# New quad orders in an attention block, and a scaled bias that stays in its tile until the MLP

## The chip, the core and the metric

The kernel runs on one core of one Trainium2 chip. The metric is the device time of one execution in microseconds; lower is better. Below, PE is TensorE's matmul stream, PEld its weight loads, DVE is VectorE, ACT is ScalarE, POOL is GpSimd and SP is SyncE, which issues nearly all DMAs.

## The reference

A transformer block over 2048 tokens of 576 channels: adaptive layer norm, attention with 32 query heads of 18 channels that share one key and one value head, then adaptive layer norm and an MLP of 4608 hidden channels with its own layer norm, all in float32.

```python
mod = (_silu(c) @ w_mod).reshape(c.shape[0], 6, 1, -1)
h = _layernorm(x) * (1 + ca) + sa
x = x + ga * attention(h)        # softmax(q k^T * 18**-0.5) v, then @ wo
h = _layernorm(x) * (1 + cb) + sb
x = x + gb * (gelu(_layernorm(h) @ w1 + b1) @ w2 + b2)
```

## The kernel before

Three stages follow each other: projections to q, k and v (until about 130 us), attention (until about 1372 us), and the MLP.

**Attention** works in 32 **quads**: quad n is four heads over one quarter of the queries (512 tokens). For each quad the kernel needs the scores (S), their row maxima, the exponential, the product with V and a normalisation. Each step that makes a bank of PSUM is one 64-row matmul of 512 columns, and there are two kinds:

- S tokens (`st_mm`, L941): a score matmul; ACT takes its exponential into P (L943).
- M, X and R tokens (`mx_mm`, L327 and L951): they find the row maxima of the quad that comes next. An M bank is reduced by DVE (L963); an X bank goes through a ReLU on ACT (L954) and is combined with an R bank on DVE (L961).

The matmuls are 64 rows high, so the array holds two of them; the digit of a token (0 or 1) is the half that it uses. Matmuls of different halves run side by side, those of one half one after the other. X and R always use half 1. A quad issues 64 S, 48 M, 8 X and 8 R.

Seven banks stand in a ring (`bank`, L80): a token takes the oldest bank, one with a plus sign the second oldest, one with two the third oldest. A matmul into a bank waits until ACT or DVE has read what was there.

V tokens (`pv_mm`, L921) are the products with V: a V token with the number g issues g parts, each of four 32-column matmuls of 128 columns, into the eighth bank, psC. They lag eight parts behind the scores; the last parts of a quad are therefore among the first of the next quad's order. When they are done, `post_quad` (L742) begins with a copy of psC to the tile O on ACT (L747). Its other steps are tokens of the next quad's order:

- T1: DVE transposes O to T (L750).
- RC: DVE takes the reciprocals (L753), POOL multiplies T by them (L754).
- T2: DVE transposes T back to O (L756).
- OS: ACT rounds O into the tile os (L766), POOL writes the remainder (L767), and SP sends both to the operand of the output projection.

O, T and os have one buffer each. The token F1 finishes the maxima of the next quad, F2 transposes them on PE (L365) and sends them to the queries of the next quad.

**The order is written by hand as a string of tokens**: QUAD for quads 0 to 8, QUADW for 9 to 30, LAST for 31. QUADW has one token more, WO: a piece of the output projection (14 matmuls on PE, L732, and an addition on DVE, L736). After every four parts of V the function `between` (L967) gives POOL steps of a preparation of the MLP's weights (L800 to L883) and, every second time, a step of a queue `fill`, which holds the second layer norm. Two steps of that norm are PE transposes (L163) and run only behind a WO, which happens in every second quad from 12 to 26. Three groups of four parts per quad, those ahead of F2 and RC, get no preparation steps.

The second bias, scaled (`load_b2` L634, `b2_scaled` L639), is made once in the attention, for the layer norm of the first two token blocks (L626), in a tile of the pool px. That pool is closed after the attention; the MLP opens a new one and makes the bias again for the other two blocks: a load ahead of its first step (L1112) and the two POOL operations of `b2_scaled` inside step v = 0 (L1421).

Of the kernel before, what the change touches and what calls it, by code (L numbers as in the profile page):

```python
# [8 lines left out]
F32 = mybir.dt.float32  # L9
# [5 lines left out]
S, D, H, DH, F = 2048, 576, 32, 18, 4608  # L15
# [17 lines left out]
def block_kernel(ctx: ExitStack, tc, x, wqkv, wo, w1, b1, w2, b2, c, wmod, ident_in, out):  # L33
# [3 lines left out]
    per = ctx.enter_context(tc.tile_pool(name="per", bufs=1))  # L37
# [27 lines left out]
    def big(): return per.tile([128, 10, 512], F32R, name="big", bufs=3)  # L65
# [387 lines left out]
    for tb in range(NB):  # L453
        nz = big() if tb + 1 < NB else None
        for i, m in enumerate((4, 0, 1, 2, 3)):
# [42 lines left out]
    px = pxp.__enter__()  # L498
# [4 lines left out]
    WO, YR, ATT, B2 = {}, {}, {}, {}  # L503
# [128 lines left out]
        yield  # L632

    def load_b2():  # L634
        b2g = px.tile([128, D], F32, name="b2g")
        sy.dma_start(b2g, b2.to_broadcast([128, D]))
        return b2g

    def b2_scaled(b2g):  # L639
        po.tensor_mul(b2g, b2g, BC[:, 2, :])  # L640
        po.tensor_scalar(b2g, b2g, 2.0, None, op0=ALU.mult)
        return b2g
# [99 lines left out]
    def post_quad(n, PV):  # L742

        tb, qd = divmod(n, NQ)
        e = po if n < NQT - 1 else ve
        O = px.tile([128, TB], F32, name="O")
        ac.activation(O, PV, AF.Copy)  # L747
        yield
        T = px.tile([128, 16, 32], F32, name="T")
        ve.transpose(T.rearrange("p a b -> p (a b)"), O)  # L750
        yield
        R = px.tile([128, 16], F32, name="R", bufs=2)
        ve.reciprocal(R, T[:, :, DH])  # L753
        e.tensor_tensor(T, T, R[:, :, None].to_broadcast([128, 16, 32]), op=ALU.mult)  # L754
        yield
        ve.transpose(O, T.rearrange("p a b -> p (a b)"))  # L756
        yield
        if tb not in ATT:
            assert tb
            ATT[tb] = big()  # L760
        A = ATT[tb].rearrange("p (s k) t -> p s k t", s=2)
        if n == NQT - 1:
            os = A[:, :, KD - 1, :]
        else:
            os = px.tile([128, 2, TB], F32R, name="os")
        ac.activation(os[:, 0], O, AF.Copy)  # L766
        e.tensor_tensor(os[:, 1], O, os[:, 0].bitcast(F32), op=ALU.subtract)  # L767
        if qd < NQ - 1:
            for j in range(4):
                k, r = divmod(4 * qd + j, HC)  # L770
                sy.dma_start(A[DH * r:DH * (r + 1), :, k, :].bitcast(F32), os[32 * j:32 * j + DH].bitcast(F32))
        elif n < NQT - 1:
            for j in range(4):
                sy.dma_start(A[DH * j:DH * (j + 1), :, KD - 1, :].bitcast(F32),
                             os[32 * j:32 * j + DH, :1].bitcast(F32).to_broadcast([DH, 2, TB]))
            for j in range(4):
                r = 4 + j % 3
                sy.dma_start(A[DH * r:DH * (r + 1), j // 3, KD - 1, :].bitcast(F32), os[32 * j:32 * j + DH, 1].bitcast(F32))
# [114 lines left out]
    QUAD = """S0+ M0 S1 S1+ M0 V3 S0 M1 S1+ M0 M1++ S0 V3 M0 S1+ M1 S0+ V2 M0 S1+ S1 M0+ X1 S0+ V4 T1 X1 M0 M1 M0
            S1 S0 V4 S1 RC M0+ S1 S0 M0+ S0+ M1 V3 S0 M1 R1 S1+ S0 M0+ X1 V3 M0 S1 S1+ R1 S0 M0 S1 V3 M0+ X1 M0
            S0 S1 S0 M1 V3 M0+ S1 S1+ M0 S0 R1+ S0 V3 R1+ S0 S1 M1 S0 M0 X1 V3 M0+ S1 M0 S1 S0 S0 R1 V3 M0+ X1
            S0+ M1 S0 M1+ V3 S1 M0+ M0 S1 T2 S0 S1 V4 M0 S1 S0 M1+ S0 M1 V3 S0 R1+ S1 M0 F1 S1 S0 V3 X1 M0 S1 M0
            R1 S0 F2 OS V4 M0+ M1 S0+ S1 M0+ X1 V4 S1 M0 S1+ S0 M1 M0+ S1 V2 R1 S0 M1 S0+ V2 S0 S1 M0 M1 V2 S1""".split()
# [443 lines left out]
    fill = deque([ln2_pair()])  # L1341
# [20 lines left out]
    for v in range(NV):  # L1362
# [6 lines left out]
        def more(half="", first="", room=False):  # L1369

            if v in (0, NG - 1, NG):
                form(first if v == 0 else half if v == NG - 1 else {"+T4": "-T4 +T1 -B22", "-T4": "-T1 -t1"}.get(first, ""))
            elif v > NG + 1 and fill:
                step(fill)
            elif 0 < v < NG and fill and (room or mark[0] != "T" or v == NG - 2):
                mark[0] = next(fill[0], "end")
                if mark[0] == "end":
                    fill.popleft()
            if v == 0 and rest:
                for _ in range(2):  # L1380
# [140 lines left out]
```

## Time and profile before

| | us |
|---|---|
| median of 3 runs | 2222.11 (2221.9 to 2223.86) |
| profiled execution, own time | 2223.82 |
| its span, first to last instruction | 2221.7 |
| PE busy | 2201.1 (99%) |
| DVE busy | 1927.8 (87%) |
| ACT busy | 1644.4 (74%) |
| POOL busy | 1525.1 (69%) |

The shares are averages over stages with different limits. PE's busy time counts matmuls in the pipeline, with modelled ends, so a busy PE is not PE at its peak. The granted clock of TensorE is 1.00 of its higher level, 2.4 GHz, in every quad shown below. Quads are found in the trace by ACT's copy of psC to O, which runs once in each; the time from one to the next is called the period.

### The profile page before, as it was taken

What the parts mean: (1) busy time and instruction counts of PE and PEld (TensorE: products, weight loads), DVE (VectorE), ACT (ScalarE), POOL (GpSimd) and SP (SyncE); (2) the same over time, 40 slices, a digit from 0 to 9 for tenths busy, and PEclk for the clock granted to TensorE, in tenths of its full rate; (3) what the DMA queues carried; (4) which work ended last, traced back from release to release, by engine and by line L of the source; (5) the groups of instructions that cost most, each with busy time, mean ns of one, the idle gap of its engine ahead of it and who ended that gap; (6) DMA issues with size and microseconds to landing.
All of it is one profiled execution on the core that took longest, in us unless ns stands there. A gap on an engine that the chain in (4) does not pass through costs nothing.

```text
span 2221.7 us, 46258 instructions
## 1 busy us (share of the span) xinstructions
PE 2201.1 (99%) x16814; PEld 1457.5 (66%) x16814; DVE 1927.8 (87%) x3417; ACT 1644.4 (74%) x3145; POOL 1525.1 (69%) x1761
## 2 busy tenths in 40 slices
PE   8999999999999999999999999999999999999999
PEld 6655555444544545445454456888888898989898
DVE  7589999999999999999999983888888878888887
ACT  5569999999999999999999998444445444343443
POOL 6654455766776786687686630988888867877776
PEclk9999999999999999999999999999999999999999
DMA  6232143433333333342333322666666646676664
GB/s 231 84 132 92 34 134 117 140 128 109 125 117 120 124 124 108 102 140 94 116 130 112 130 70 69 204 178 175 177 181 179 184 131 182 179 219 188 178 184 124
DMA packets 183880, 308.01 MB, mean 139 GB/s; under 512 B 18815, under 2 KB 74511, under 8 KB 183653
## 3 DMA queue, kind: packets, MB, share of 16 engines
q1 hardware_dynamic: 183509, 304.91, 44.1%
q8 instruction: 133, 2.18, 0.4%
q14 instruction: 94, 0.77, 0.1%
q10 hardware_dynamic: 144, 0.15, 0.0%
HBM read 200.97 MB, written 93.79 MB: 133 GB/s over the span
## 4 chain that ended last, share of the span: by engine, by line
PE 88%; POOL 2%; DVE 2%; ACT 1%; issue 1%; DMA 0%; POOLq 0%; ACTq 0%
PE psC L931 22%; PE psB L1159 18%; PE psA L1262 16%; PE bk L941 15%; PE bk L327 10%; PE bk L732 2%; PE bk L951 2%; PE psA L1296 1%; DVE mx L963 1%; ACT P L943 1%; PE psA L732 0%; POOL r L801 0%; PE psB L256 0%; POOL r L862 0%; DVE mx L352 0%
## 5 line engine op out<-in xcount | busy, mean ns | idle before, releaser
L943 ACT ACTIVATE P<-bk 128x512 f32<-128x512 f32 x2048 | 1065.6, 625 | 34.6 <-PE bk L327 11.6
L963 DVE TENSOR_REDUCE mx<-bk 128x1 f32<-128x512 f32 x1476 | 935.0, 681 | 43.9 <-PE bk L327 30.8
L941 PE MATMUL bk<-qst,KS 64*128 64x512 f32 x2048 | 596.4, 432 | 1.2 <-DVE mx L345 0.8
L327 PE MATMUL bk<-KS,qst 64*128 64x512 f32 x1722 | 593.5, 438 | 0.8
L931 PE MATMUL psC<-P,V 128*32 128x256 f32 (+3 forms) x6784 | 569.1, 433 | 0.0
L941 PEld LDWEIGHTS bk<-qst,KS 64*128 64x128 f32 x2048 | 296.7, 185 | 266.0 <-ACT P L943 143.0
L1159 PE MATMUL psB<-ops,w1a 128*128 128x512 f32 x1512 | 393.8, 396 | 0.2 <-DVE h L1174 0.2
L327 PEld LDWEIGHTS bk<-KS,qst 64*128 64x128 f32 x1722 | 272.7, 185 | 130.3 <-ACT P L943 57.9
L1159 PEld LDWEIGHTS psB<-ops,w1a 128*128 128x128 f32 x1512 | 270.1, 188 | 46.6 <-DVE h L1174 0.6
L931 PEld LDWEIGHTS psC<-P,V 128*32 128x32 f32 x6784 | 152.7, 108 | 191.6 <-issue 159.3
L1268 DVE TENSOR_TENSOR XT<-psA,XT 128x576 f32<-128x576 f32 x330 | 241.7, 753 | 20.2 <-PE psA L1262 14.8
L1262 PEld LDWEIGHTS psA<-w2s,big 128*128 128x128 f32 x1584 | 223.0, 188 | 15.5 <-POOL big L1236 3.6
L1262 PE MATMUL psA<-w2s,big 128*128 128x288 f32 x1584 | 230.9, 295 | 1.0 <-POOL big L1236 0.8
L1172 ACT ACTIVATE psB<-gs 128x512 f32<-128x512 f32 x144 | 86.7, 602 | 127.9 <-DVE gs L1171 127.9
L1236 POOL TENSOR_TENSOR big<-s,big 128x512 fp32r<-128x512 f32 x132 | 171.0, 1295 | 10.6
L1168 ACT ACTIVATE h<-psB,b1t 128x512 f32<-128x512 f32 x144 | 98.0, 680 | 102.0 <-PE psB L1159 79.6
L961 DVE CUSTOM_DVE_ANT_0 xc<-bk,xc 128x512 f32<-128x512 f32 x246 | 167.3, 680 | 3.1 <-PE bk L327 1.7
L954 ACT ACTIVATE xc<-bk 128x512 f32<-128x512 f32 x246 | 152.9, 622 | 1.6 <-PE bk L327 1.5
L767 POOL TENSOR_TENSOR os<-O,os 128x512 fp32r<-128x512 f32 x31 | 39.9, 1287 | 139.0 <-ACT os L766 136.6
L1171 DVE SCALAR_TENSOR_TENSOR gs<-psB,h 128x512 f32<-128x512 f32 x144 | 98.5, 684 | 38.5 <-ACT psB L1169 38.3
L801 POOL TENSOR_TENSOR r<-r,r 128x256 fp32r<-128x256 f32 (+1 forms) x162 | 121.8, 752 | 13.0
L1177 ACT ACTIVATE big<-h 128x512 fp32r<-128x512 f32 x39 | 24.7, 633 | 133.9 <-DVE h L1174 133.9
(219 smaller groups left out, 3277.1 us busy)
## 6 DMA issues: line engine op xcount, KB each, us to landing
w1a<-w1scr SPq DMA_DIRECT2D x252, 256.0 KB
w2s<-w2sum SPq DMA_DIRECT2D x132, 288.0 KB
w1scr<-r SPq DMA_DIRECT2D x126, 256.0 KB
w2s<-w2scr SPq DMA_DIRECT2D x76, 288.0 KB
w2scr<-r SPq DMA_DIRECT2D x72, 288.0 KB
w2sum<-r SPq DMA_DIRECT2D x72, 288.0 KB
qst<-qscr SPq DMA_DIRECT2D x192, 72.0 KB
w1a<-w2scr SPq DMA_DIRECT2D x33, 288.0 KB
```

The costliest lines, as they stand in the source:

```text
L327: pe.matmul(o, QST[n][64 * g:64 * g + 64, p, 128 * qt:128 * (qt + 1)], KS[64 * g:64 * g + 64, 512 * kb:512 * (kb + 1)], start=True, stop=True)
L801: po.tensor_tensor(o[:, n:2 * n], src, o[:, :n].bitcast(F32), op=ALU.subtract)
L931: pe.matmul(PVt[n][32 * j:32 * (j + 1), cs], V[:, kc, :], t[:, j, cs], start=(kc == 0 and h0 == 0), stop=(kc == 15), skip_group_check=True)
L941: pe.matmul(t, KS[64 * g:64 * g + 64, 128 * kc:128 * (kc + 1)], QST[n][64 * g:64 * g + 64, i, :], start=True, stop=True)
L943: ac.activation(P[n, kc][:, 2 * i + g, :], t, AF.Exp, scale=SCALE)
L954: ac.activation(XC[-1], t, AF.Relu)
L961: ve.tensor_tensor_reduce(c, t, c, 1.0, -3.0e38, ALU.add, ALU.max, o)
L963: ve.tensor_reduce(o, t, axis=AX.X, op=ALU.max)
L1159: pe.matmul(o, x, y, start=(first and i == 0), stop=(i == len(terms) - 1), skip_group_check=True)
L1236: po.tensor_tensor(unit(u, 1), x, unit(u, 0).bitcast(F32), op=ALU.subtract)
L1262: pe.matmul(p[:, i, :288], x[:, ts_], W2S[k][:, y], start=(bool(first) and q == 0), stop=(q == 2), skip_group_check=True)
L1268: ve.tensor_tensor(o, p[:, :, :288], o, op=ALU.add)
```

## The change

Three edits. QUAD and QUADW are other strings with the same tokens; LAST stays. In `post_quad` the tile for the attention's output may now be made by steps of `fill` that run at that point, where it was asserted before; this concerns quad 1 alone. The bias tile comes from the pool `per`, which lives through the whole program, and the second load and the second scaling are gone.

```diff
     def load_b2():
-        b2g = px.tile([128, D], F32, name="b2g")
+        b2g = per.tile([128, D], F32, name="b2g")
...
         if tb not in ATT:
-            assert tb
-            ATT[tb] = big()
+            while not tb and tb not in ATT:
+                step(fill)
+            if tb not in ATT:
+                ATT[tb] = big()
...
-    QUAD = """S0+ M0 S1 S1+ M0 V3 S0 M1 S1+ M0 M1++ S0 V3 M0 S1+ M1 S0+ V2 M0 S1+ S1 M0+ X1 S0+ V4 T1 X1 M0 M1 M0
...
+    QUAD = """M1++ S0 S1+ S1 M0 V3 M0 X1 M0+ S0 S1 M0+ S1 V2 S0+ M1 S0+ R1 V3 S0 M1 M0 S1+ S0 S1 M0 V4 M0+ S1 S0
...
-            M1 S1+ S0 M0 S1 M0 V3 R1 S1 M0 M1+ S0 S1+ S0 V4 S1 T2 OS M0 X1++ M0 S1+ M0 WO S0 M1 S0 M1 S0 M1 V3
...
+            M0 S1 M0 S0+ S1 M0 V3 F2 S1 M0 X1 M0 M1 S0 V4 M1 S0 S1 M0 X1 M0+ V4 S1 S0+ R1 T2 S0 R1 M0 OS WO""".split()
...
-    B2["b"] = load_b2()
...
-        if v == 0:
-            b2_scaled(B2["b"])
```

The new strings move instructions at three places that the prediction speaks of. The first is PE around the output projection, in the quad with the second piece. L941 is a score matmul, L327 and L951 are maxima, L732 is the projection, L931 (L934 after the change) a product with V. Before:

```order
L951 MATMUL bk_7638<-KD_82,qst 128x512
L327 MATMUL bk_7642<-KS,qst 128x512
L941 MATMUL bk_7646<-qst,KS 128x512
L327 MATMUL bk_7649<-KS,qst 128x512
L732 MATMUL bk_7652<-wos,big 128x288 x14
L941 MATMUL bk_7668<-qst,KS 128x512
L327 MATMUL bk_7671<-KS,qst 128x512
L941 MATMUL bk_7674<-qst,KS 128x512
L327 MATMUL bk_7677<-KS,qst 128x512
L941 MATMUL bk_7680<-qst,KS 128x512
L327 MATMUL bk_7683<-KS,qst 128x512
L931 MATMUL psC<-P,V 32x256 x4
```

After the change (L944 is the score matmul now), where the projection is the last token of the quad:

```order
L327 MATMUL bk_7933<-KS,qst 128x512
L944 MATMUL bk_7937<-qst,KS 128x512
L327 MATMUL bk_7940<-KS,qst 128x512
L327 MATMUL bk_7943<-KS,qst 128x512
L732 MATMUL bk_7953<-wos,big 128x288 x14
L327 MATMUL bk_7969<-KS,qst 128x512
L327 MATMUL bk_7972<-KS,qst 128x512
L944 MATMUL bk_7976<-qst,KS 128x512
L327 MATMUL bk_7979<-KS,qst 128x512
L944 MATMUL bk_7982<-qst,KS 128x512
L944 MATMUL bk_7985<-qst,KS 128x512
L934 MATMUL psC<-P,V 32x512 x4
```

Before, a score followed the projection at once, and the block closed with V of three parts; now two maxima come first, and the block, which runs over from one quad to the next, closes with V of four.

The second place is POOL between its multiplication of T (L754) and the remainder of os (L767, L769 after the change), in the same quad; the other rows are the preparation of the MLP's weights. Before:

```order
L754 TENSOR_TENSOR T<-T,R 128x512
L840 TENSOR_TENSOR w2b<-r_6785,w2b 128x288
L800 CAST r_7586<-w2b 128x288
L801 TENSOR_TENSOR r_7586<-w2b,r_7586 128x288
L767 TENSOR_TENSOR os<-O,os 128x512
```

After the change:

```order
L754 TENSOR_TENSOR T<-T,R 128x512
L802 CAST r_7731<-r_7181 128x256
L803 TENSOR_TENSOR r_7731<-r_7181,r_7731 128x256
L802 CAST r_7766<-r_7181 128x256
L803 TENSOR_TENSOR r_7766<-r_7181,r_7766 128x256
L802 CAST r_7801<-r_7181 128x256
L803 TENSOR_TENSOR r_7801<-r_7181,r_7801 128x256
L864 TENSOR_TENSOR r_7639<-r_7181 128x256
L802 CAST r_7899<-r_7639 128x256
L803 TENSOR_TENSOR r_7899<-r_7639,r_7899 128x256
L769 TENSOR_TENSOR os<-O,os 128x512
```

The two were four rows apart and are ten rows apart: RC moved from 24 parts of V into the quad to 36, OS from 34 to the end, behind all 64.

The third is POOL at the start of the MLP (ops are operands of its first layer, gt of its second, s the sums from which others are made). Before:

```order
L1072 TENSOR_TENSOR ops<-yr,ops 128x1024 x2
L640 TENSOR_TENSOR b2g<-b2g,BC 128x576
L641 TENSOR_SCALAR b2g<-b2g 128x576
L1179 CAST gt_21144<-h 128x512
L1180 TENSOR_TENSOR gt_21144<-h,gt_21144 128x512
L1179 CAST gt_21144<-h 128x512
L1180 TENSOR_TENSOR gt_21144<-h,gt_21144 128x512
L1238 TENSOR_TENSOR s<-h 128x512
```

After the change:

```order
L1075 TENSOR_TENSOR ops<-yr,ops 128x1024 x2
L1181 CAST gt_21178<-h 128x512
L1182 TENSOR_TENSOR gt_21178<-h,gt_21178 128x512
L1181 CAST gt_21178<-h 128x512
L1182 TENSOR_TENSOR gt_21178<-h,gt_21178 128x512
L1240 TENSOR_TENSOR s<-h 128x512
```

The two operations on the bias are gone; all that stood behind them follows the operands at once.

## Rows read from the trace of the kernel before

**Rows 1.** The page, parts 1 and 4: busy time; the chain that ended last.
```profile
PE 2201.1 (99%) x16814; PEld 1457.5 (66%) x16814; DVE 1927.8 (87%) x3417; ACT 1644.4 (74%) x3145; POOL 1525.1 (69%) x1761
...
PE 88%; POOL 2%; DVE 2%; ACT 1%; issue 1%; DMA 0%; POOLq 0%; ACTq 0%
```

**Rows 2.** Windows, one quad each: span, busy us (instructions) by engine, clock, DMA.
```profile
285.98:323.48 37.50, 37.50 (x363) 18.94 (x361) 36.60 (x71) 37.08 (x76) 22.44 (x32) 1.00 0.40 135
...
552.95:593.15 40.20, 40.13 (x353) 19.70 (x353) 37.57 (x76) 37.49 (x77) 37.08 (x52) 1.00 0.42 136
...
672.24:712.35 40.11, 40.01 (x358) 19.76 (x358) 37.99 (x77) 38.07 (x78) 23.90 (x32) 1.00 0.35 116
...
791.43:831.52 40.09, 40.02 (x353) 19.64 (x353) 37.54 (x76) 37.47 (x76) 36.59 (x51) 1.00 0.43 139
...
1187.95:1226.94 38.99, 38.99 (x353) 19.46 (x353) 36.88 (x73) 37.44 (x76) 23.73 (x35) 1.00 0.31 106
```

**Rows 3.** Timeline of PE, QUADW: start us, us, engine, line, operation.
```profile
1193.46 0.49 PE L941 MATMUL bk<-qst,KS 64*128 64x512 f32 x1
...
1194.58 1.07 PE L931 MATMUL psC<-P,V 128*32 128x512 f32 x8
...
1195.57 0.49 PE L941 MATMUL bk<-qst,KS 64*128 64x512 f32 x1
...
1196.69 0.85 PE L931 MATMUL psC<-P,V 128*32 128x384 f32 x8
...
1197.47 0.50 PE L941 MATMUL bk<-qst,KS 64*128 64x512 f32 x1
```

**Rows 4.** Timeline of PE, QUADW, the output projection and the small transpose.
```profile
1201.62 0.50 PE L941 MATMUL bk<-qst,KS 64*128 64x512 f32 x1
...
1202.52 2.13 PE L732 MATMUL bk<-wos,big 126*128 126x288 f32 x14
...
1204.57 0.49 PE L941 MATMUL bk<-qst,KS 64*128 64x512 f32 x1
...
1216.43 0.28 PE L365 MATMUL bk<-ident,mxf 128*16 128x128 f32 x1
```

**Rows 5.** Waits: engine and line, waited for, us in total, times, longest.
```profile
PEld psC L931 <- issue: 159.3, 570, 0.4
```

**Rows 6.** Timeline of POOL, DVE, PE at the MLP's start.
```profile
1393.81 1.43 POOL L640 TENSOR_TENSOR b2g<-b2g,BC 128x576 f32<-128x576 f32 x1
...
1395.34 1.67 POOL L641 TENSOR_SCALAR b2g<-b2g 128x576 f32<-128x576 f32 x1
...
1398.44 0.69 DVE L1174 SCALAR_TENSOR_TENSOR h<-psB,h 128x512 f32<-128x512 f32 x1
...
1400.84 1.31 POOL L1238 TENSOR_TENSOR s<-h 128x512 f32<-128x512 f32 x1
...
1404.23 1.59 PE L1262 MATMUL psA<-w2s,big 128*128 128x288 f32 x10 [0.81 <-POOL big L1236]
```

**Rows 7.** Timeline of DVE and ACT in the quad from 552.95.
```profile
568.70 0.71 DVE L756 STREAM_TRANSPOSE O<-T 128x512 f32<-128x512 f32 x1 [1.18 <-POOL T L754]
...
569.44 0.63 ACT L766 ACTIVATE os<-O 128x512 fp32r<-128x512 f32 x1 [1.65 <-DVE O L756]
```

**Rows 8.** Timeline of PE, QUAD, in its run of blocks of seven.
```profile
292.64 0.86 PE L931 MATMUL psC<-P,V 128*32 128x128 f32 x16
...
296.60 0.85 PE L931 MATMUL psC<-P,V 128*32 128x384 f32 x8
```

**Rows 9.** O and os: ACT's timeline, the page's group, POOL's waits in QUADW.
```profile
1187.95 0.60 ACT L747 ACTIVATE O<-psC 128x512 f32<-128x512 f32 x1
...
1202.64 0.62 ACT L766 ACTIVATE os<-O 128x512 fp32r<-128x512 f32 x1
...
L767 POOL TENSOR_TENSOR os<-O,os 128x512 fp32r<-128x512 f32 x31 | 39.9, 1287 | 139.0 <-ACT os L766 136.6
...
POOL r L800 <- DMA w1scr<-r: 27.4, 12, 6.3
```

More of the change, by code (lines that the diff above doesn't have):

```diff
@@ L892, in block_kernel @@
     LAG = 8
-    QUAD = """S0+ M0 S1 S1+ M0 V3 S0 M1 S1+ M0 M1++ S0 V3 M0 S1+ M1 S0+ V2 M0 S1+ S1 M0+ X1 S0+ V4 T1 X1 M0 M1 M0
[L894 to L897, printed above, removed]
@@ L898, in block_kernel @@
-    QUADW = """S1+ M0 M0 X1 S0 X1 M0 V3 S1 M0 M0+ S1 R1 S0+ V2 M1 S0 M0 S1+ S0 R1+ V3 M0 X1+ S0 S1+ S0+ M1 V4 S0 T1
-            M1+ S0 S1 M0 S1+ V4 S1 M0 M1 S0 S1+ M0 V4 S1 M0 S1 S0+ M1 S0 R1 V4 S1 M0 M0 RC X1+ S0 M1+ S1 V3 S0
-            M1 S1+ S0 M0 S1 M0 V3 R1 S1 M0 M1+ S0 S1+ S0 V4 S1 T2 OS M0 X1++ M0 S1+ M0 WO S0 M1 S0 M1 S0 M1 V3
-            S1 S0 M1 S0 M0 X1 V3 S1 M0 M1+ M0 S1+ S0 V4 M0 S1+ S0 S1 S0+ R1+ M0 V4 S0+ S1 M0 M1++ M1 S0+ V3 S0
-            R1 M0+ F1 S1 S0 X1+ V4 M0 S1 M0 S1+ S0+ M1 F2 V3 S0+ R1 S0+ S1 M0 S1 M0 V3 M0 X1 S1 M0+ S1 R1+ S0 V3""".split()
+    QUAD = """M1++ S0 S1+ S1 M0 V3 M0 X1 M0+ S0 S1 M0+ S1 V2 S0+ M1 S0+ R1 V3 S0 M1 M0 S1+ S0 S1 M0 V4 M0+ S1 S0
+            S1 M0 M1+ V3 S0 M1+ S1 M0 S0+ S1 V3 S0 T1 M1 X1 M0 M1 S0 V4 S0 R1 S0 M1 M0 S1+ V3 S1 S0 S1 M0 S0 M1+
+            V3 S1 M0 M0++ S1 M0++ X1 V4 S1 M0+ RC S0 M0 X1 S0+ M1 V3 R1 S0 S1 S0 M0 S1+ M0 V3 M1+ S0 R1 M0+ S1
+            S0+ X1 V3 M0+ S1 S1++ S1 M0+ M0 X1 V3 M1+ S0 S1 M0+ S1 T2 S0 V3 S0 R1+ M0 R1 S0 S1 OS V4 M1 M0+ X1
+            S0++ M1 S0+ F1 S1 V4 M0 S1+ M0 S1 M0+ S1 F2 V3 S0+ R1 S0+ X1 M0+ S1 M1 V3 S0 R1 M0 M1+ S0 S1+ S0 V3
+            S1 M0""".split()
@@ new lines, in block_kernel @@
+    QUADW = """M1 M0+ S0 M1 S0 S1 V4 M1 S0 S1+ M0++ M1 S0+ S1 V4 S1+ M0 S0 S1 M0+ M0 T1 S1 V4 M1+ S0 M0++ S1 S0 X1
+            V5 S0 M1+ X1 M1+ M0 S1 S0 V3 S0 M1 R1 S1 S0+ M0 S1 V3 M0 S1 M0+ S1 S0 M1 S0 V3 S0+ M1 S1+ M0 R1 S1
+            S0 V3 M0 S1 M0 S0 S1+ M0 S1 V4 M0+ S1 M0+ X1 M1 S0 S1 V3 S0+ R1 RC X1+ S0 S0+ M1 M0 V3 X1 M0 R1 M0++
+            S1 S0 S1 V4 S1 S0 X1++ M0 S0+ M0 R1 V4 S0 M1++ M0 S1++ S1 M0 S1 V3 R1 S0 S0+ M0 M1 S0 F1 S1 V3 S1+
+            M0 S1 M0 S0+ S1 M0 V3 F2 S1 M0 X1 M0 M1 S0 V4 M1 S0 S1 M0 X1 M0+ V4 S1 S0+ R1 T2 S0 R1 M0 OS WO""".split()
```

## The prediction

> **What bounds the kernel now.** I read four views in this order: the page, windows of single quads, PE's timeline, and the waits.
>
> The page says PE is busy 99% of the span and the chain that ended last lies on PE for 88% [rows 1]. A busy PE can still be waiting for a bank, so this alone proves nothing about the attention.
>
> The windows show what a quad costs [rows 2]. In QUAD a period is 37.50 us, with ACT busy 37.08 and DVE 36.60. In QUADW a plain period is 38.99 us, with ACT busy only 37.44. A quad that also has the layer norm's transposes (358 instructions on PE, not 353) takes 40.11. Two quads without transposes, from 552.95 and from 791.43, still take 40.20 and 40.09. So ACT has 0.42 us of slack in QUAD and 1.55 in QUADW, and something else sets the pace in QUADW.
>
> PE's timeline says what. I call a **block** the bank matmuls between two V tokens with the V token that ends them. Matmuls of different halves run side by side, so I count **passes**: a block of seven with three in one half and four in the other needs four. From 1193.46 to 1194.58 such a block takes 1.12 us to its V, and the next one, from 1195.57 to 1196.69, again 1.12 [rows 3]. Six matmuls in three passes take 0.90, from 1201.62 to 1202.52 [rows 4]. A pass is therefore 0.22 us, with 0.24 fixed. A V of four parts takes 0.99 us to the next matmul (1194.58 to 1195.57), one of three 0.78 (1196.69 to 1197.47) [rows 3]: 0.21 a part, 0.15 fixed. A block costs **0.39 + 0.22 x passes + 0.21 x parts**. The fixed part is mostly the change between the two shapes of matmul: 570 times, some 18 per quad, the weight load for V waits 159.3 us in all on nothing that the profile shows [rows 5], 0.28 us each. The projection takes 2.05 us from 1202.52 to 1204.57, and opens a second 0.24 in its block [rows 4].
>
> I counted blocks and passes in the strings, in order and with the wrap from one quad to the next. Every quad has 64 parts, 13.44 us.
>
> - QUAD before: 21 blocks, 68 passes: 8.19 + 14.96 + 13.44 = 36.59 us. Seen 37.50, so 0.91 over.
> - QUADW before: 19 blocks, 68 passes, and 2.29 for the projection: 38.10. Seen 38.99, so 0.89 over.
>
> The small transpose behind F2, 0.28 us [rows 4], is in both; some 0.6 us a quad is waiting for banks. PE's own order is thus nearly the whole of a period.
>
> **The change part by part.** The sums are made against the profiled execution, 2223.82 us, which lies 1.7 above the median of 2222.11.
>
> *Blocks and passes.* QUAD becomes 20 blocks with 69 passes: 7.80 + 15.18 + 13.44 = 36.42, or -0.17 a quad and **-1.5** for nine quads. QUADW becomes 18 blocks with 71 passes: 7.02 + 15.62 + 13.44 + 2.29 = 38.37, or +0.27 a quad and **+5.9** for 22. The new QUADW has one change of shape fewer but more blocks of seven, in which the fourth pass is half empty.
> Each change of shape shows as its own wait before V [rows 5]. The Trainium skill says the same (TensorEngine Tiling (Array Packing), Key Properties): changing the tiling mode drains the engine. By that rule alone, one block fewer in 31 quads, the sum of this part would be -0.39 x 31 = -12 us. The trace does show the drain, but also the price of the passes, 0.22 each, which the rule leaves out.
>
> *Waits for banks.* I laid the no-wait durations above along each string and noted how long a bank has between one matmul into it and the next. In QUADW before, 20 of some 130 come back within 1.75 us; in the new one 9. The maxima's banks that come back so soon go from 8 to 4. The threshold is a choice: the matmul itself is 0.5 us [rows 3], a drain such as ACT's copies 0.6 [rows 9], and one more ahead of it in the queue 0.5 (ACT's 76 instructions of a quad fill 37.08 us [rows 2]). If the 0.61 us of waits shrink with that count, 0.34 a quad go, **-7.4** for 22. Nothing shows the new waits, so the ends are 0 (none of them goes) and -13.4 (all go). In QUAD the count goes from 30 to 32; I take 0 there, with -2.3 as the better end: with -0.17 already counted, ACT's slack of 0.42 leaves 0.25 for nine quads.
>
> *The late transpose.* In the quad from 552.95 DVE waits 1.18 us at T2 for POOL's multiplication, ACT then 1.65 for DVE [rows 7]; PE's period is 1.2 over the plain one, and from 791.43 it is 1.1 over [rows 2]. In the new QUADW 28 parts of V lie between RC and T2, not 10, and POOL has ten rows there, not four, mostly casts and subtractions: T is ready long before. Both stalls go: **-2.3**. What is late next is os, see below.
>
> *Quads with transposes.* They still stand behind WO, in the same eight quads, 1.1 us dearer than plain ones [rows 2]. I take 0, with 3 us either way, since two extra banks turn the ring against the string's pluses.
>
> *The bias.* POOL loses 1.43 + 1.67 us at the start of the MLP [rows 6]. Its subtraction at 1400.84 needs an h that DVE ends at 1399.13 (1398.44 + 0.69), so the chain behind it can start 1.7 us earlier; PE waits 0.81 at its end, at 1404.23 [rows 6]. The wait is the smaller: **-0.8**, with 0 and -1.0 as ends. The missing load of the bias, the tile's new pool and the `fill` step in quad 1 I count at nothing: the load has its whole stage to land, POOL and SP in quad 1 do the same steps one token earlier.
>
> Sum: -1.5 + 5.9 - 7.4 - 2.3 - 0.8 = -6.1 us, so 2217.7 by the profiled execution and **2216.0** by the median.
>
> **The rivals.**
>
> *All waits go.* QUAD falls to ACT's 37.08 (-0.42 x 9 = -3.8), QUADW to 38.37 + 0.28 (-0.34 x 22 = -7.5); with -2.3 and -0.8 that is -14.4: 2207.7. For it: the new blocks are more uniform, so ACT and DVE get like portions. Against it: QUAD before is fairly uniform too, and waits 0.6 us a quad. Chance 0.18.
>
> *The waits stay.* -1.5 + 5.9 - 2.3 - 0.8 = +1.3: 2223.4, no change. For it: the threshold of 1.75 us is mine. Chance 0.22.
>
> *Slower: ACT sets the pace in the blocks of seven.* In QUAD two blocks of seven with three parts take 3.96 us, 292.64 to 296.60, so 1.98 each [rows 8], where PE alone needs 0.39 + 0.88 + 0.63 = 1.90. Each gives ACT four drains of nearly 0.5. The new QUADW has nine such blocks, four in a row, the old one five. Four more at 0.08 are 0.32 a quad, +7.0; if the waits of the old string stay besides, the sum is +8.3: 2230.4. It decides once ACT has no gap left over from the longer blocks to make up the 0.08. Against it: in rows 3 such a block follows a longer one and takes the plain 1.12 to its V. Chance 0.18.
> The Trainium skill (Perfetto Trace Analysis, Identifying the Most-Contended Engine) would pick this rival, since for ScalarE it takes the busy share as a fair measure of the distance to the limit; here that share is 99% in QUAD and 96% in QUADW.
>
> *Slower: the copy to O waits for POOL.* O has one buffer, and POOL reads it for os. In the old QUADW os is rounded at 1202.64, and the next copy to O came 24.3 us later, at 1226.94 [rows 2, 9]. Now only the projection and two blocks lie between, some 2.05 + 0.90 + 0.99 + 1.12 + 0.99 = 6.05 us. POOL needs 1.29 for the remainder [rows 9]; it decides if more than about 4 us of other work stand ahead of it. POOL has waited for the store of a weight tile 12 times in these quads, up to 6.3 us [rows 9]. One us late in each of 22 quads would give -6.1 + 22: 2238. Against it: POOL mostly stands waiting for os, 136.6 us in all [rows 9]. Chance 0.06.
>
> **How the numbers follow.** My forecast has 0.36. About 0.2%, 4.4 us, is what a measurement of this kernel can tell from no change: faster is below 2217.7, slower above 2226.5. The forecast's own range, 2211 to 2222, holds mostly faster times (0.32) and some equal ones (0.04). Faster: 0.32 + 0.18 = 0.50. Same: 0.04 + 0.22 = 0.26. Slower: 0.18 + 0.06 = 0.24. The range goes from 2205, past the case in which all waits go, to 2231, past ACT's pace; the copy to O lies outside.
>
> **What would show it.** Right: plain QUADW periods of about 38.9, QUAD of about 37.3, no quad at 40 without transposes, no wait of DVE for POOL's T, PE's wait at the MLP's start gone. Wrong: plain periods of 39.3 and more with ACT's idle time below 1.2 us (ACT's pace) or ACT waiting for POOL ahead of the copy to O.

## The result, and the profile after

The changed kernel takes 2229.81 us (median of 6 runs, 2228.19 to 2231.12), the kernel before 2222.24 beside it (6 runs, 2220.45 to 2224.24). The ratio is 1.0033, interval 1.0020 to 1.0046: **slower by some 7.5 us**, where 2216.0 and "faster" had been forecast. The profiled execution took 2230.95 us with a span of 2229.2; before it was 2223.82 and 2221.7, so the profiles differ by 7.1 and the spans by 7.5.

| | before | after |
|---|---|---|
| first copy to O | 172.82 us | 173.06 |
| QUAD, typical period | 37.45 | 37.4 to 37.6, once 38.75 |
| passage from QUAD to QUADW | 38.56 | 38.57 |
| QUADW, plain | 39.0 | 39.36 to 39.39 |
| QUADW, with the norm's statistics (eight) | 39.0 | 39.79 |
| QUADW, with the transposes (eight) | 40.1 | 40.1 |
| last copy to O, to the end of the span | 849.96 | 848.61 |

The page of the changed kernel, parts 1 and 4, answers to [rows 1]:

```profile
PE 2207.9 (99%) x16886; PEld 1479.3 (66%) x16886; DVE 1925.6 (86%) x3417; ACT 1639.1 (74%) x3145; POOL 1522.0 (68%) x1759
...
PE 96%; DVE 1%; DMA 1%; POOL 1%; ACT 1%; issue 1%; SPq 0%; ACTq 0%; POOLq 0%; DVEq 0%
```

PE's part of the last chain rose from 88 to 96%, and yet the time is longer: whatever else had been on the chain went, and what PE itself does between two copies to O grew. The windows of single quads, with the columns of [rows 2], show where:

```profile
248.60:287.35 38.75, 37.53 (x371) 18.81 (x371) 36.42 (x71) 37.02 (x76) 13.37 (x13) 1.00 0.24 74
324.74:362.33 37.59, 37.59 (x371) 18.72 (x371) 36.40 (x71) 36.92 (x76) 25.89 (x38) 1.00 0.36 118
437.18:475.75 38.57, 36.87 (x354) 17.99 (x353) 35.98 (x70) 36.11 (x75) 27.24 (x41) 1.00 0.37 124
634.36:674.15 39.79, 39.79 (x355) 20.23 (x352) 38.30 (x77) 37.28 (x76) 26.16 (x37) 1.00 0.33 112
674.15:714.23 40.08, 40.08 (x360) 21.00 (x357) 37.20 (x72) 37.89 (x78) 31.07 (x42) 1.00 0.32 106
1272.69:1312.06 39.37, 39.37 (x355) 20.50 (x352) 36.81 (x71) 37.29 (x76) 22.12 (x33) 1.00 0.36 119
```

The last row is a plain QUADW, 0.38 us above the 38.99 of [rows 2]. The QUAD period of 38.75 and the passage of 38.57 are the only ones whose span and PE's busy time differ by more than 0.01, by 1.22 and 1.70: there PE stands still. (Before, the passage took as long without standing still; it is a shorter piece of the order now, 354 instructions on PE, not 367.) Of the pair in the middle, the first holds the norm's statistics on DVE (busy 38.30) and the second the transposes. Added up from copy to copy, the 7.5 us are: start 0.2, QUAD and the passage to QUADW 0.9, QUADW 6.0, the last two quads 1.7, the rest -1.35.

SP's queue near the end of quad 8 tells what PE waited for. Its rows give the start of a run of DMA issues and its length; L371 sends the finished maxima (`qst<-ms`) to the next quad's queries, the others are the transfers of os. The changed kernel:

```profile
462.15 3.50 SPq L776 DMA_DIRECT2D big<-os  x4
465.75 3.08 SPq L780 DMA_DIRECT2D big<-os  x4
468.93 1.28 SPq L371 DMA_DIRECT2D qst<-ms  x2
```

The kernel before, same quad:

```profile
462.80 1.33 SPq L371 DMA_DIRECT2D qst<-ms  x2
464.23 3.32 SPq L774 DMA_DIRECT2D big<-os  x4
```

DVE and PE of the changed kernel there:

```profile
465.60 0.27 DVE L368 SCALAR_TENSOR_TENSOR ms<-bk,ms 16x128 fp32r<-16x128 f32 x1
...
471.53 0.47 PE L944 MATMUL bk<-qst,KS 64*128 64x512 f32 x1 [1.70 <-DMA qst<-ms]
```

The maxima are ready at 465.87, but eight issues for os stand ahead of them on SP, the last four of which begin at 465.75; so they go out at 468.93, 3.06 us later. The new QUAD has the token OS ahead of F2, the old one behind it. The prediction never looked at that order.

### The profile page after: what moved, and what is told of

It reads as the page before. It is cut to its first block, busy times and chain, and to the rows that moved or that the text cites. A ratio compares the mean times of both kernels' runs of the same rounds, so it can differ in the third digit from the quotient of the medians.

```text
span 2229.2 us, 46406 instructions
## 1 busy us (share of the span) xinstructions
PE 2207.9 (99%) x16886; PEld 1479.3 (66%) x16886; DVE 1925.6 (86%) x3417; ACT 1639.1 (74%) x3145; POOL 1522.0 (68%) x1759
## 4 chain that ended last, share of the span: by engine, by line
PE 96%; DVE 1%; DMA 1%; POOL 1%; ACT 1%; issue 1%; SPq 0%; ACTq 0%; POOLq 0%; DVEq 0%
PE psC L934 23%; PE psB L1161 18%; PE psA L1264 16%; PE bk L944 15%; PE bk L327 12%; PE bk L732 2%; PE psB L256 2%; PE bk L954 2%; PE psA L1298 1%; PE psA L327 1%; PE psA L732 1%; DMA bigw<-in_wqkv 1%; PE psB L163 0%; DVE mx L352 0%; DMA qscr<-qs 0%
## 5 line engine op out<-in xcount | busy, mean ns | idle before, releaser
L944 PE MATMUL bk<-qst,KS 64*128 64x512 f32 x2048 | 618.8, 440 | 3.0 <-DMA qst<-ms 1.7
L327 PE MATMUL bk<-KS,qst 64*128 64x512 f32 x1722 | 563.7, 436 | 0.5 <-DVE mx L345 0.4
L934 PE MATMUL psC<-P,V 128*32 128x128 f32 (+3 forms) x6856 | 561.9, 429 | 0.0
L944 PEld LDWEIGHTS bk<-qst,KS 64*128 64x128 f32 x2048 | 311.3, 184 | 209.2 <-ACT P L946 83.8
L327 PEld LDWEIGHTS bk<-KS,qst 64*128 64x128 f32 x1722 | 263.0, 184 | 157.6 <-DVE mx L966 72.4
L934 PEld LDWEIGHTS psC<-P,V 128*32 128x32 f32 x6856 | 158.6, 108 | 201.8 <-issue 175.8
L769 POOL TENSOR_TENSOR os<-O,os 128x512 fp32r<-128x512 f32 x31 | 39.8, 1284 | 185.1 <-ACT os L768 185.1
```

What stands on the lines that cost most here:

```text
L327: pe.matmul(o, QST[n][64 * g:64 * g + 64, p, 128 * qt:128 * (qt + 1)], KS[64 * g:64 * g + 64, 512 * kb:512 * (kb + 1)], start=True, stop=True)
L934: pe.matmul(PVt[n][32 * j:32 * (j + 1), cs], V[:, kc, :], t[:, j, cs], start=(kc == 0 and h0 == 0), stop=(kc == 15), skip_group_check=True)
L944: pe.matmul(t, KS[64 * g:64 * g + 64, 128 * kc:128 * (kc + 1)], QST[n][64 * g:64 * g + 64, i, :], start=True, stop=True)
```

## The experiments

Unless said otherwise, an edit is to the kernel before, or to the changed one, as named.

**One part of the change at a time** (5 to 11 runs each; the kernel before 2223.25 in 27).

*b2_only*: the kernel before with the bias edit alone.

```diff
-        b2g = px.tile([128, D], F32, name="b2g")
+        b2g = per.tile([128, D], F32, name="b2g")
...
-    B2["b"] = load_b2()
...
-        if v == 0:
-            b2_scaled(B2["b"])
```

> The kernel before with the bias edit alone. Theory: POOL's 3.1 us ahead of the second layer's operands go and with them PE's wait of 0.81 us at the MLP's start, so 0.8 to 1.4 us faster than before (in the changed kernel's trace the stretch behind the last copy to O is 1.35 us shorter). Rival: the wait moves to the operand that comes next, and the time stays within 0.3 us.

Measured: 2221.8 us, ratio 0.9994 (0.9985 to 1.0003), the end 849.36 after the last copy to O, not 849.96. PE's wait of 0.81 at the MLP's start [rows 6] is gone; the matmul has no bracket behind it any more:

```profile
1402.01 1.74 PE L1261 MATMUL psA<-w2s,big 128*128 128x288 f32 x12
```

It follows that the term of -0.8 had its mechanism right. Its size is better read from all the profiles of this case, since the stretch behind the last copy to O differs in them by the bias alone: the six kernels that make the bias twice take 849.96 to 850.71 us there, the eight that make it once 848.48 to 849.36, one profile each. The medians, 850.04 and 848.58, lie 1.5 us apart; b2_only's own profile shows the smallest gain, 0.6. The times of b2_only alone can't tell it from nothing. Where it exceeds the wait of 0.81, no run here shows why.

*quad_only*: the kernel before with the new string QUAD and the `while not tb` step in `post_quad`; QUADW and the bias as before.

> The kernel before with the new string QUAD alone. Theory: the string itself is nearly neutral (-0.1 us a quad), but OS now comes ahead of F2, so the rows of maxima stand on SP's queue behind the transfers of os; where that queue is longer (quad 2, and quad 8 with eight transfers of os) the first scores of the next quad wait 1.2 and 1.7 us. Sum +1 to +3 us. Rival: the quads lose nothing to that queue, and the time is 1 to 2 us below the kernel before.

Measured: 2226.4 us, ratio 1.0014 (1.0005 to 1.0023). The periods in QUAD are 37.4 to 38.3, and the passage to QUADW takes 42.66 where it took 38.56. SP, PE and a window of it:

```profile
464.31 3.07 SPq L780 DMA_DIRECT2D big<-os  x4
467.48 1.28 SPq L371 DMA_DIRECT2D qst<-ms  x2
```

```profile
470.10 0.76 PE L944 MATMUL bk<-qst,KS 64*128 64x512 f32 x1 [1.98 <-DMA qst<-ms]
```

```profile
470.00:475.00 5.00, 4.90 (x21) 2.25 (x21) 2.56 (x4) 2.69 (x6) 3.36 (x7) 0.50 0.78 246
```

The new QUAD is no gain by itself. Its maxima stand behind os on SP here too, PE waits 1.98 us, and over the next 5 us the granted clock is 0.50, the level of 1.2 GHz, so that a bank matmul takes 0.76 where it takes 0.50.

*quadw_only*: the kernel before with the new string QUADW alone.

> The kernel before with the new string QUADW alone. Theory: three more passes for one block fewer (+0.27 us a quad), with waits for banks that do not shrink since ACT or DVE sets the pace of the blocks of seven (+0.1), and another +0.4 in the eight quads with the layer norm's statistics, against 3 us from the late transpose and 3 us from the quads with transposes: +5 to +8 us. Rival: most of the loss of the whole change is in QUAD's queue, and this kernel is within 2 us of the kernel before.

Measured: 2230.17 us, ratio 1.0035 (1.0021 to 1.0049): about as much as the whole change loses. The parts don't add up exactly: +6.9, +3.2 and -1.5 by these medians are 8.6, not 7.6, and quad_only loses 4.1 at the passage to the old QUADW, where the changed kernel loses nothing (38.57 against 38.56). A plain quad, window as above:

```profile
512.09:551.46 39.37, 39.37 (x355) 20.50 (x352) 36.80 (x71) 37.28 (x77) 19.71 (x30) 1.00 0.34 115
```

*f2_first*: the changed kernel with OS in QUAD moved from ahead of F2 to directly behind it.

```diff
-            S0+ X1 V3 M0+ S1 S1++ S1 M0+ M0 X1 V3 M1+ S0 S1 M0+ S1 T2 S0 V3 S0 R1+ M0 R1 S0 S1 OS V4 M1 M0+ X1
-            S0++ M1 S0+ F1 S1 V4 M0 S1+ M0 S1 M0+ S1 F2 V3 S0+ R1 S0+ X1 M0+ S1 M1 V3 S0 R1 M0 M1+ S0 S1+ S0 V3
+            S0+ X1 V3 M0+ S1 S1++ S1 M0+ M0 X1 V3 M1+ S0 S1 M0+ S1 T2 S0 V3 S0 R1+ M0 R1 S0 S1 V4 M1 M0+ X1
+            S0++ M1 S0+ F1 S1 V4 M0 S1+ M0 S1 M0+ S1 F2 OS V3 S0+ R1 S0+ X1 M0+ S1 M1 V3 S0 R1 M0 M1+ S0 S1+ S0 V3
```

> The changed kernel with the token OS of QUAD moved to directly behind F2, so that the rows of maxima go out ahead of os. Theory: the two waits of 1.2 and 1.7 us go and nothing else changes: 2 to 3.5 us faster than the changed kernel, 4 to 5.5 us slower than the kernel before. Rival: the scores of the next quad were waiting for a bank, not for the rows, and the time stays that of the changed kernel, 7 to 8 us slower than before.

Measured: 2227.03 us, ratio 1.0018 (1.0010 to 1.0027). On SP the maxima now go first, and both stalls are gone:

```profile
464.58 1.34 SPq L371 DMA_DIRECT2D qst<-ms  x2
466.02 3.32 SPq L776 DMA_DIRECT2D big<-os  x4
```

```profile
249.02:286.44 37.42, 37.42 (x371) 19.02 (x371) 36.40 (x71) 36.79 (x77) 16.60 (x16) 1.00 0.18 52
436.20:473.44 37.24, 37.24 (x354) 18.26 (x353) 35.97 (x70) 36.08 (x74) 28.16 (x40) 1.00 0.33 110
```

Each is 1.33 us shorter than in the changed kernel (38.75 and 38.57). So 2.7 us of the 7.5 are the place of OS on SP's queue. With that mended, QUAD still runs at 37.4, as before the change.

**Taking the load off ACT and DVE** (one execution each). Six kernels halve what ACT or DVE does in the attention, while PE issues the same matmuls, so that with both halved what is left of a period is close to PE's own order.

*before_both*, *after_both*: both halved, in the kernel before and in the changed one. The products then read the first 128 columns of P again and again, the exponential and the maxima half of theirs. The edit (a kernel with one engine halved has its part of it alone; the scale is changed where the maxima are cut):

```diff
-            pe.matmul(PVt[n][32 * j:32 * (j + 1), cs], V[:, kc, :], t[:, j, cs],
+            pe.matmul(PVt[n][32 * j:32 * (j + 1), cs].rearrange("p (a b) -> p a b", b=128), V[:, kc, :], t[:, j, None, :128].to_broadcast([128, h1 - h0, 128]),
...
-        ac.activation(P[n, kc][:, 2 * i + g, :], t, AF.Exp, scale=SCALE)
+        ac.activation(P[n, kc][:, 2 * i + g, :256], t[:, :256], AF.Exp, scale=0.01 * SCALE)
...
-            ve.tensor_reduce(o, t, axis=AX.X, op=ALU.max)
+            ve.tensor_reduce(o, t[:, :256], axis=AX.X, op=ALU.max)
```

> The kernel before with exponentials and reductions both on half of their columns. The count of blocks and passes gives 38.38 us for a plain QUADW and 36.87 for a QUAD, so the new QUADW is 0.27 us dearer by its passes alone and the new QUAD 0.17 cheaper. Rival: passes cost nothing of their own, the new QUADW is then cheaper here by the block that it saves, 0.39 us.

> The changed kernel with exponentials and reductions both on half of their columns, so that no bank is waited for: PE's order alone. Both theories: the count of blocks and passes, 38.65 us for a plain QUADW and 36.70 for a QUAD. Rival: the count misses something, and the periods differ from it by more than 0.2 us.

Measured: 2200.18 and 2204.83 us. A plain QUADW and a QUAD of the kernel before so changed, then of the changed kernel:

```profile
505.78:544.17 38.39, 38.39 (x353) 17.83 (x353) 26.32 (x76) 25.04 (x75) 22.84 (x30) 1.00 0.32 108
...
282.47:319.31 36.84, 36.84 (x363) 16.42 (x363) 24.92 (x70) 25.28 (x76) 22.91 (x32) 1.00 0.43 138
```

```profile
544.97:583.75 38.78, 38.78 (x353) 18.60 (x353) 26.82 (x77) 25.56 (x76) 34.07 (x46) 1.00 0.35 114
...
283.15:319.88 36.73, 36.73 (x371) 16.95 (x371) 24.70 (x70) 25.27 (x75) 24.12 (x36) 1.00 0.42 138
```

This is the test of the count of blocks and passes. It said 38.10 + 0.28 = 38.38 for the old QUADW, and 38.39 came; for the new 38.37 + 0.28 = 38.65, and 38.73 to 38.78 came (quads with the norm's statistics, such as the one from 544.97, take no longer than plain ones here). By PE's order alone the new QUADW is dearer by 0.37, not 0.27, and the new QUAD cheaper by 0.11. And it splits the periods: in a plain quad, waits are 38.99 - 38.39 = 0.60 before and 39.37 - 38.75 = 0.62 after. **They did not shrink.** Over all 21 periods of QUADW they are 15.5 us before, leaving out the stalls at T2, and 16.5 after: the quads with the statistics wait more (39.79 - 38.73 = 1.06, where it was 0.60), those with the transposes less (40.10 - 39.52 = 0.58, where it was 40.10 - 39.14 = 0.96).

*after_act*, *before_act*: ACT halved alone (exponential and products). *after_dve*, *before_dve*: DVE halved alone (maxima).

> The changed kernel with the exponentials on half of their columns (256 of 512; the products with V then read the first 128 columns of each part several times, so PE's work is the same). Theory: ACT sets the pace in the blocks of seven, so the plain QUADW period falls from 39.37 us to PE's own count, 38.65 to 38.85. Rival: DVE's reductions set it, and the period stays above 39.2.

> The kernel before, with ACT's exponential over the first 256 of 512 score columns and the PV matmuls reading the first 128 columns of P again for each part (that part of the attention is left out; PE's instructions and passes stay). With both engines halved the plain QUADW period was 38.38 us against 38.99, so 0.61 us of waits are to be shared out. In the changed kernel ACT alone accounted for 0.39 to 0.41 of its 0.60. Theory A (the early reuses of banks made the old waits, as the prediction said, and ACT's pace makes the new ones): ACT's share here is smaller, about 0.3 (the five blocks of seven), and plain QUADW falls to about 38.7. Theory B (both kernels lose the same to ACT's pace, and early reuses cost nothing): ACT's share is again 0.4, plain QUADW at 38.58 to 38.60. QUAD under both: from 37.45 to about 37.0.

> The changed kernel with the reductions of the M banks on half of their columns, and the scores scaled by 0.01 ahead of the exponential, which keeps them finite. Theory (ACT's pace): the plain QUADW period stays at 39.2 to 39.4 us, and only the surplus of the quads with the layer norm's statistics (39.79) goes, since that is DVE's. Rival (DVE's pace): 38.65 to 38.85 us.

> The kernel before, with the maxima of the scores taken over the first 256 of 512 columns (that part is left out; scores are scaled by 0.01 before the exponential so that sums stay finite; ACT's work is whole). Theory A: DVE has no share of the old waits of its own, plain QUADW 38.9 to 39.0. Theory B: the same. A rival: DVE's maxima hold the early reused banks, then plain QUADW falls by 0.2 to 0.4, to 38.6 to 38.8. Under all, the two quads with a late multiplication on POOL stay at 39.4 to 40.2.

Measured: 2215.48, 2213.45, 2227.3 and 2219.5 us. Of after_act a plain QUADW and one with the statistics; of before_act a plain QUADW and a QUAD; of after_dve a plain quad and one with the statistics; of before_dve a plain one:

```profile
507.56:546.53 38.97, 38.97 (x353) 18.90 (x353) 36.79 (x72) 25.45 (x75) 19.70 (x30) 1.00 0.35 116
...
625.81:665.43 39.62, 39.60 (x353) 18.95 (x353) 38.21 (x78) 25.54 (x75) 26.28 (x36) 1.00 0.34 113
```

```profile
1256.78:1295.40 38.62, 38.62 (x353) 18.34 (x353) 36.84 (x72) 25.14 (x75) 22.06 (x35) 1.00 0.30 105
...
284.91:321.86 36.95, 36.95 (x363) 17.07 (x363) 36.50 (x71) 25.25 (x76) 22.80 (x32) 1.00 0.41 135
```

```profile
515.57:554.93 39.36, 39.36 (x355) 19.59 (x352) 24.97 (x71) 37.29 (x76) 19.71 (x30) 1.00 0.33 115
554.93:594.28 39.35, 39.35 (x355) 19.61 (x352) 26.85 (x77) 37.29 (x76) 34.63 (x46) 1.00 0.35 114
```

```profile
947.01:985.97 38.96, 38.96 (x353) 18.96 (x353) 26.32 (x74) 37.43 (x76) 35.50 (x50) 1.00 0.37 127
```

ACT alone accounts for 39.37 - 38.97 = 0.40 of the new 0.62 and for 38.99 - 38.62 = 0.37 of the old 0.60. Over the three plain periods that both kernels have at the same place (the first of QUADW, the last, and the last but two) ACT's share is 0.40 to 0.43 after and 0.34 to 0.39 before, and what is left without it 0.17 to 0.25 and 0.22 to 0.26. These are single executions, and the two kernels differ by hardly more than their quads do among themselves. So theories A and B on record are not told apart; what is left without ACT fell by less than 0.1 us a quad, not by 0.34. DVE alone holds nothing in plain quads. In the eight quads with the statistics it is the larger part: 39.79 becomes 39.35 with DVE halved, 39.62 with ACT halved, 38.73 with both. QUAD, with ACT halved, falls from 37.45 to 36.95 although DVE is whole: there ACT is the bound.

The place is seen in PE's timeline of the changed kernel, at the starts of V tokens that end blocks of seven with three parts each:

```profile
1277.71 0.85 PE L934 MATMUL psC<-P,V 128*32 128x384 f32 x8
...
1279.68 0.85 PE L934 MATMUL psC<-P,V 128*32 128x384 f32 x8
...
1281.63 0.86 PE L934 MATMUL psC<-P,V 128*32 128x128 f32 x16
```

The same in after_both, then in after_act:

```profile
550.15 0.85 PE L934 MATMUL psC<-P,V 128*32 128x384 f32 x8
552.06 0.85 PE L934 MATMUL psC<-P,V 128*32 128x384 f32 x8
553.96 0.86 PE L934 MATMUL psC<-P,V 128*32 128x128 f32 x16
```

```profile
1263.97 0.85 PE L934 MATMUL psC<-P,V 128*32 128x384 f32 x8
1265.87 0.85 PE L934 MATMUL psC<-P,V 128*32 128x384 f32 x8
1267.79 0.86 PE L934 MATMUL psC<-P,V 128*32 128x128 f32 x16
```

Spacings are 1.97 and 1.95 in the changed kernel, 1.91 and 1.90 with both halved, 1.90 and 1.92 with ACT halved; with DVE halved the same blocks still take 1.97 and 1.96. So each such block loses 0.05 to 0.06 us to ACT, as QUAD's blocks may have done [rows 8], and nine of the new plain quad's seventeen spacings lie at 1.95 to 1.98. ACT's busy time says the same, taken over that run of blocks and not over the whole quad:

```profile
1273.17:1302.89 29.72, 29.72 (x286) 15.19 (x285) 27.69 (x55) 29.51 (x61) 17.25 (x28) 1.00 0.36 122
```

ACT is busy for 29.51 of 29.72 us; nearly all of its idle time in the quad comes behind that, around the projection.

**Can the late transpose be had alone?** (11 and 5 runs; the kernel before 2222.5 in 15.) Two kernels take the kernel before with the bias edit and move one token of the old QUADW, or two.

*best_rc*: RC two V tokens earlier. *best_t2*: T2 behind the block that holds the projection, OS one block further.

```diff
-            M1+ S0 S1 M0 S1+ V4 S1 M0 M1 S0 S1+ M0 V4 S1 M0 S1 S0+ M1 S0 R1 V4 S1 M0 M0 RC X1+ S0 M1+ S1 V3 S0
+            M1+ S0 S1 M0 S1+ V4 S1 M0 RC M1 S0 S1+ M0 V4 S1 M0 S1 S0+ M1 S0 R1 V4 S1 M0 M0 X1+ S0 M1+ S1 V3 S0
```

```diff
-            M1 S1+ S0 M0 S1 M0 V3 R1 S1 M0 M1+ S0 S1+ S0 V4 S1 T2 OS M0 X1++ M0 S1+ M0 WO S0 M1 S0 M1 S0 M1 V3
-            S1 S0 M1 S0 M0 X1 V3 S1 M0 M1+ M0 S1+ S0 V4 M0 S1+ S0 S1 S0+ R1+ M0 V4 S0+ S1 M0 M1++ M1 S0+ V3 S0
+            M1 S1+ S0 M0 S1 M0 V3 R1 S1 M0 M1+ S0 S1+ S0 V4 S1 M0 X1++ M0 S1+ M0 WO S0 M1 S0 M1 S0 M1 V3
+            S1 T2 S0 M1 S0 M0 X1 V3 S1 OS M0 M1+ M0 S1+ S0 V4 M0 S1+ S0 S1 S0+ R1+ M0 V4 S0+ S1 M0 M1++ M1 S0+ V3 S0
```

> The kernel before with the scaled bias kept in its tile as in the change, and in QUADW the reciprocal's token RC moved two V blocks earlier, so that POOL's multiplication of O starts some 2.5 us earlier. Theory: the stalls of the four quads that take 39.35 to 40.20 (a transposed copy that waited for POOL's product) go, 0.4 + 1.2 + 1.1 + 0.4 = 3 us, and the bias another 0.6 to 1.4: about 2219 us, ratio 0.9982. Rival: what held POOL is its own earlier queue (the other multiplications and selects), not the time at which RC releases it; then the stalls stay and only the bias's 1.4 is seen (2221.8).

> The kernel before with the bias edit, and in QUADW the transposed copy of O (T2) moved behind the block with the output projection, about 5 us later, and OS one more block later; RC stays. Theory: with 5 us more DVE no longer waits for POOL, the four slow quads fall to 39.0, gain 3 us + 1.4 for the bias: about 2219 us, ratio 0.9982. Rival: OS now lands its transfers nearer to F2's maxima rows on SP's queue, which then wait behind them as they did in the changed kernel's QUAD (1.3 us each time): periods of 40 and over turn up in other quads, 2222 to 2226 us.

Measured: best_rc 2219.41 us, ratio 0.9986 (0.9978 to 0.9995), **faster than both kernels**: 3.1 us less than the kernel before, of which the bias is some 1.5. best_t2 2229.54 us, ratio 1.0035 (1.0022 to 1.0049). The two quads of best_rc that had taken 40.20 and 40.09 [rows 2], and the transpose that had waited 1.18 [rows 7]:

```profile
552.31:591.30 38.99, 38.99 (x353) 19.60 (x353) 37.55 (x76) 37.60 (x77) 36.72 (x51) 1.00 0.44 147
...
789.58:828.58 39.00, 39.00 (x353) 19.62 (x353) 37.55 (x76) 37.59 (x76) 35.37 (x50) 1.00 0.42 140
```

```profile
566.76 0.66 DVE L756 STREAM_TRANSPOSE O<-T 128x512 f32<-128x512 f32 x1
```

Three of the four slow quads take 39.0 now; the first stays at 39.35, and no DVE wait for T stands in it. That one has another cause, on DVE: with DVE halved it takes 38.94 (before_dve). best_t2 lost its stalls too, but for 0.24 us in each of the two larger ones, and its quads became 0.34 to 0.47 dearer, by neither theory on record. A window of it, DVE and PE:

```profile
873.59:913.03 39.44, 39.38 (x353) 19.39 (x353) 37.52 (x76) 37.44 (x76) 34.95 (x50) 1.00 0.38 128
```

```profile
890.32 0.46 DVE L736 TENSOR_TENSOR XT<-bk,XT 128x288 f32<-128x288 f32 x1 [0.43 <-PE bk L732]
890.78 1.89 DVE L963 TENSOR_REDUCE mx<-bk 128x1 f32<-128x512 f32 x3
892.59 0.70 DVE L756 STREAM_TRANSPOSE O<-T 128x512 f32<-128x512 f32 x1
```

```profile
892.80 0.85 PE L931 MATMUL psC<-P,V 128*32 128x384 f32 x8
...
894.95 1.06 PE L931 MATMUL psC<-P,V 128*32 128x512 f32 x8
```

DVE adds the projection's result, and three maxima later it has the transpose as well. PE's block there takes 894.95 - 892.80 = 2.15 us from V to V; in best_rc, where the transpose lies 2.3 us ahead of that addition, the same block takes 1.69:

```profile
887.86 0.85 PE L931 MATMUL psC<-P,V 128*32 128x384 f32 x8
...
889.55 1.06 PE L931 MATMUL psC<-P,V 128*32 128x512 f32 x8
```

So in this quad the 0.46 is lost in the one block where the transpose now stands among DVE's maxima; that a late maximum holds PE there is read from the order of DVE's jobs, and no run moves the transpose alone.

## Why the prediction was wrong

| step | predicted, us | measured, us | by |
|---|---|---|---|
| QUADW, blocks and passes | +5.9 | +7.7 (0.37 x 21 periods) | after_both, before_both |
| QUAD, blocks and passes | -1.5 | -0.4 | seven periods, less the stall of 1.33; ACT bounds them |
| waits in QUADW | -7.4 | +0.9 (16.5 against 15.5) | after_both, before_both |
| the late transpose | -2.3 | -2.7 | three quads of 39.4 to 40.2 |
| quads with the norm | 0 | in the rows above | a pair is dearer by some 0.8, twice a plain 0.38 |
| bias | -0.8 | -1.35 | from the last copy to O to the end |
| os ahead of the maxima on SP | not seen | +2.7 | f2_first |
| start, passage, last two quads | not seen | +0.6 (0.2 - 1.3 + 1.7) | from copy to copy |
| sum | -6.1 | +7.5 | profile against profile +7.1, spans +7.5 |

**The step that failed most is "if the 0.61 us of waits shrink with that count, 0.34 a quad go".** The size of the waits (0.61) was right to 0.01. Reading their cause off the number of banks that come back within 1.75 us was not. The count fell from 20 to 9, and the waits of a plain quad went from 0.60 to 0.62. More than half of them were ACT's before (0.34 to 0.39) and still are (0.40 to 0.43). ACT's share is not a matter of single short returns: over the 29.72 us of the new string's blocks of seven ACT has no gap to speak of, and each such block with three parts takes 0.05 to 0.06 longer than with ACT halved. What makes the other 0.2 us, before and after, stays open. The rival "ACT sets the pace in the blocks of seven" named this and priced a block at 0.08. It had 0.18, and should have been ahead of the forecast, since [rows 8] showed the same blocks taking 1.98 in QUAD.

That rival's time, 2230.4, is within 1 us of the measured one, but by luck: it added 7.0 us of new waits, where the waits of QUADW rose by 0.9, and it lacked 1.8 us of the passes and the 2.7 us on SP. Of its sign only half showed. Plain periods are 39.3 and more, but ACT's idle time in them is 39.37 - 37.29 = 2.08 us, not below 1.2: a mean over the quad hides that ACT is full for three quarters of it. The rival "the waits stay" had the waits right in kind; its 2223.4 misses by the passes, QUAD and the place of os.

The Trainium skill (Perfetto Trace Analysis, Identifying the Most-Contended Engine) takes ScalarE's busy share for a fair measure of its distance to the limit. In QUAD the runs agree: ACT at 99%, and halving it gives 0.50 us. In QUADW the share of 95% hides that 0.40 of 0.62 us of waits are ACT's.

**The second step that failed was an omission:** the prediction spoke of OS against the copy to O and never of OS against F2, though both issue on SP. The copy to O did not wait for POOL, as said; the maxima waited for os.

**The third was small.** The new QUADW's passes are dearer than counted by some 0.1 us: 38.73 to 38.78 with both engines halved, not 38.65. Its blocks of seven with three parts take 1.90 to 1.91 bare, where 1.90 was counted, those with four 2.11 to 2.13, where it was 2.11. It has 14 blocks of seven where the old one had 8; 0.01 to 0.02 for each of the six more would make up the 0.1, but no run separates that. Over 21 periods it is the 1.8 us between +5.9 and +7.7.

The sign of that term was right against the rule it was weighed with. By the Trainium skill's rule alone (TensorEngine Tiling (Array Packing), Key Properties) that a change of tiling mode drains the engine, one change of shape fewer per quad would have been worth an estimated -0.39 each, the fixed part of a block. The runs show +0.37 in QUADW: the three passes more cost more than the block saved. The wait row [rows 5] is a poor count of such drains, though: after the change it reads

```profile
PEld psC L934 <- issue: 175.8, 649, 0.4
```

with 31 blocks fewer. In the plain quad of 1272.69 four of its 21 entries lie inside V tokens of four or five parts, where they cost PE nothing: the V of five takes 1.21 us, and 0.15 + 5 x 0.21 gives 1.20.

The last two quads (+1.7) and the passage from QUAD to QUADW (-1.3 with F2 in front) belong together: in the new strings the copy to O falls at another token, and the periods at both ends shift (354 instructions on PE in the passage, not 367, and 328, not 306, in the first of the last two). That leaves +0.4.

## What to carry to other kernels

Count a hand-written order in blocks and passes first: with the other engines' load halved that count was right to 0.1 us in 39, and it says that blocks of seven matmuls over two halves waste half a pass each. Then ask which engine empties the banks at its full rate, and over which stretch, since a share over the whole quad hid it here; while ACT did, less than half as many early returns gained nothing that could be measured. Halving an engine's work in a trial tells it in one run. And when a token moves, go through every queue it issues on: the issues for os held two small transfers back by 3.06 us on SP, and PE with them.

## What was not expected of the hardware

Waits of PE for the rows of maxima ended differently. In the changed kernel PE waited 1.70 us at 471.53, and the granted clock stayed at 1.00 (the level of 2.4 GHz) in the 5 us behind it. In quad_only it waited 1.98 us at 470.10, and the clock was 0.50 (1.2 GHz) in the 5 us behind it, so that PE, busy for 4.90 of them, did about half its work there; by estimate that is some 2.5 us. The passage took 42.66 us, 4.1 more than in the kernel before, wait and slow clock together. The length of the wait alone does not decide it. In after_dve PE waited only 1.49 us at 281.50, and the clock behind it fell as well:

```profile
281.50 0.50 PE L944 MATMUL bk<-qst,KS 64*128 64x512 f32 x2 [1.49 <-DMA qst<-ms]
```

```profile
281.50:286.50 5.00, 5.00 (x39) 2.50 (x39) 1.70 (x4) 3.75 (x7) 1.09 (x2) 0.66 0.81 251
```

That quad took 40.40 us, where the changed kernel's took 38.75. Later in the same run a wait of 1.76 us, at 472.01, left the clock at 1.00. So here a fall of the clock came with some of these waits and not with others, and in after_dve it cost about as much as the wait.

And issuing is not free. The Trainium skill (DMA: Bandwidth & Descriptors, Issuing engines are not separate DMA queues) says that starting DMAs from several engines only saves the sequencer's time for starting them, usually small beside the transfer. Here SP's time for eight starts was 3.50 + 3.08 = 6.6 us, and just that time decided when the next transfer could go. Nor was it small beside the transfer: of the 2.60 us from the start of the two issues for the maxima, at 468.93, to the matmul that waited for them, at 471.53, SP's time for starting them is 1.28.
